# A two-layer linear-attention and MLP kernel on one core: a centred first tile, one more chunk divided in token order, two MLP tiles turned by DMA, and the orders arranged anew

## The chip, the core and the metric

The kernel runs on one core of one Trainium2 chip, in one launch. The core has five instruction streams: TensorE (PE, matmuls; its weight loads are shown apart as PEld), VectorE (DVE), ScalarE (ACT), GpSimd (POOL) and SyncE (SP), which here only issues DMAs. The metric is device time in microseconds (us), the median of the runs; lower is better. The profile is that of one more execution of the same program.

## What is computed

x is 2048 x 512 in bf16. Two layers follow one another, each an attention block and an MLP block with a residual, with the same weights in both layers:

```python
phi = lambda t: jnp.where(t > 0, t + 1, jnp.exp(t)) + 1e-6
def attention(x):                 # x is layer-normed, D = 512, 32 heads of 16
    q, k, v = heads(x @ wqkv)
    kv = einsum("sd,se->de", phi(k), v);  z = sum over s of phi(k)
    return (phi(q) @ kv / (phi(q) @ z + 1e-6)) @ wo
def mlp(x):                       # x is layer-normed, F = 1792
    return gelu_tanh(x @ w1 + b1) @ w2 + b2
for layer in range(2):
    x = x + attention(layernorm(x))
    x = x + mlp(layernorm(x))
```

Layer norm takes the mean off each row and divides by the root of the variance + 1e-5; there is no learned scale.

## The kernel before

**Tiles.** The 2048 rows are 16 tiles of 128 rows, in four chunks of four (tile 4c+k is the k-th of chunk c). A row tile is 128 x 512; matmuls contract over 128 partitions, so a product with a 512-deep weight is four matmuls into one PSUM bank, 512 columns each.

**Names.** The kernel first lists every operation as a node with a name, then plays the nodes, engine by engine, in an order that is written out by hand as long strings in `CONF["ORDER"]`. `CONF["PLACES"]` says which buffer slot each tile takes and who had it before, and `CONF["WAY"]` picks, operation by operation, the engine (`pe` or `dma` for a transpose, `dve`, `act` or `pool` elsewhere). From the data and slot dependences the waits are derived; nothing is scheduled at run time. The names that matter, with L the layer (0 or 1), t a tile, c a chunk:

| name | what | line |
|---|---|---|
| `warm` | matmuls on a constant while the first loads are under way | L747 |
| `stats`, `aggr`, `veps`, `pow`, `nmr`, `norm` + `A`/`B` L_t | layer norm ahead of attention (A) or of the MLP (B): row statistics (DVE), 1/sqrt(variance) (POOL), normalised tile in bf16 (DVE or ACT) | L773-L795 |
| `PT..`, `tc..` | a tile turned (128 x 128 blocks) on PE into PSUM, and copied out by ACT | L817, L827 |
| `T..`, `TP..` | a tile turned by a DMA that SP issues; TP turns a divided tile of queries | L804, L1067 |
| `K` L_t, `exp/relu/min/phi k..` | keys of a tile (4 matmuls), and phi of them into `pkb` | L866, L837-L854 |
| `Q` L_c_k | queries of a chunk: turned (L896), or in token order (L883) | |
| `G` | y^T phi(k), summed over all tiles; `KV` and `M` then multiply it by the weights of v and of `wo` | L958, L987, L1008, L1031 |
| `Z`, `zs`, `zb`, `dz`, `ZR` | the sums z and what is made of them | L941-L1022 |
| `D`, `ln`, `rec`, `pr` | the denominators of a chunk on turned queries: one matmul, then Ln and Exp(-) on ACT, then a product | L1074-L1082 |
| `pz`, `red`, `den`, `rec`, `pr` | the same in token order: a product with z, a sum per head, a reciprocal, a product (DVE, POOL), and then TP | L1051-L1067 |
| `WO`, `RA` | attention's output and its residual | L1097, L1102 |
| `W1`, `gelu`, `W2`, `RB`, `b2`, `OD` | the MLP, the residual, the bias, the store of a tile | L1127-L1175 |

**Stages.** Layer 0 begins with `warm`, while SP and ACT load x (tile 0 first, then tiles 1 to 3) and the weights of the keys. Tiles 0 to 5 are turned on PE, tiles 6 to 15 by DMA from SP's queue. A tile's K, phi and G follow; Q of chunks 0 and 1 fills PE. When the last tile is through, G is copied, and KV, M and the first WO form a chain through DVE and ACT, which Q of chunks 2 and 3 and the D matmuls fill. Chunks 2 and 3 are divided in token order, chunks 0 and 1 on turned queries. Then the MLP goes chunk by chunk, with W1 of chunk 0 in two halves of two tiles (256 columns), and a tile of layer 1 starts with its norm, T and K as soon as its RB is done. Layer 1 goes the same way (chunk 0 on turned queries, 1 to 3 in token order); there TB1_0 and TB1_1 are turned on PE and all other MLP tiles by DMA. The last row tile's W2 is done in two halves of 256 columns, so that its store can begin early.

**Queues.** SP issues its DMAs in the order of its string: a DMA that waits holds back those behind it. The late weights (`wv`, `wo`, `w1`, `w2`) are issued by POOL and wait until all of layer 0's first transposes have landed.

Of the kernel before, what the change touches and what calls it, by code (L numbers as in the profile page):

```python
# [1329 lines left out]
```

## Time and profile before

| | us |
|---|---|
| median of 3 runs (lowest, highest) | 328.95 (328.55, 329.53) |
| the profiled execution, its own time | 327.5 |
| its span, from the first to the last instruction | 326.3 |
| PE busy, of the span | 322.2 |
| DVE, ACT, POOL busy | 211.0, 193.1, 152.5 |
| granted TensorE clock, mean | 1.00 |

A line of a view by groups reads: line of the kernel, engine, operation, output<-inputs, partitions x elements, count; then busy time in all and the mean of one in ns; then the engine's idle time just before and what ended it. The chain of waits follows the work that ended last backwards: start, length, what. Matmuls are pipelined: the time from one to the next is shorter than the time that a row gives for one. Times in the views count from the start of the span.

### The profile page before, as it was taken

What the parts mean: (1) busy time and instruction counts of PE and PEld (TensorE: products, weight loads), DVE (VectorE), ACT (ScalarE), POOL (GpSimd) and SP (SyncE); (2) the same over time, 40 slices, a digit from 0 to 9 for tenths busy, and PEclk for the clock granted to TensorE, in tenths of its full rate; (3) what the DMA queues carried; (4) which work ended last, traced back from release to release, by engine and by line L of the source; (5) the groups of instructions that cost most, each with busy time, mean ns of one, the idle gap of its engine ahead of it and who ended that gap; (6) DMA issues with size and microseconds to landing.
All of it is one profiled execution on the core that took longest, in us unless ns stands there. A gap on an engine that the chain in (4) does not pass through costs nothing.

```text
span 326.3 us, 4763 instructions
## 1 busy us (share of the span) xinstructions
PE 322.2 (99%) x1723; PEld 159.3 (49%) x1723; DVE 211.0 (65%) x503; ACT 193.1 (59%) x334; POOL 152.5 (47%) x224
## 2 busy tenths in 40 slices
PE   8999999999999999999999999999999999999997
PEld 3444445576454444444444444458644444444444
DVE  5987679996938685142436899999989983300112
ACT  4988769797661416529673477969833454551600
POOL 5662548588663417300757434783856593100000
PEclk9999999999999999999999999999999999999999
DMA  7355753334012210331011110012034322200102
GB/s 266 120 83 97 219 189 104 105 64 68 16 32 50 54 26 3 80 64 34 0 32 33 34 32 0 19 32 50 17 82 94 69 48 66 64 0 2 64 0 80
DMA packets 46883, 20.37 MB, mean 62 GB/s; under 512 B 41932, under 2 KB 45388, under 8 KB 46860
## 3 DMA queue, kind: packets, MB, share of 16 engines
q1 hardware_dynamic: 44572, 13.00, 18.8%
q0 software_dynamic: 1056, 4.72, 4.5%
q10 hardware_dynamic: 1232, 2.36, 2.0%
q8 instruction: 13, 0.21, 0.3%
q14 instruction: 10, 0.08, 0.1%
HBM read 8.00 MB, written 2.10 MB: 31 GB/s over the span
## 4 chain that ended last, share of the span: by engine, by line
PE 97%; DVE 1%; ACT 1%; issue 0%
PE ps L1127 30%; PE ps L1163 29%; PE ps L1097 9%; PE ps L866 8%; PE ps L883 5%; PE ps L987 4%; PE ps L958 4%; PE ps L896 2%; PE ps L747 2%; PE ps L1150 1%; PE ps L1074 1%; PE ps L1008 1%; PE ps L1031 1%; PE ps L941 1%; PE ps L817 0%; DVE pkb L854 0%
## 5 line engine op out<-in xcount | busy, mean ns | idle before, releaser
L1132 ACT ACTIVATE gT<-ps,b1c 128x512 bf16<-128x512 f32 (+1 forms) x140 | 77.1, 600 | 65.3 <-PE ps L1127 65.0
L1127 PE MATMUL ps<-t,w 128*128 128x512 bf16 (+1 forms) x560 | 102.2, 336 | 0.0
L1163 PE MATMUL ps<-w,gT 128*128 128x512 bf16 x434 | 97.6, 379 | 0.0
L1127 PEld LDWEIGHTS ps<-t,w 128*128 128x128 bf16 x560 | 54.6, 98 | 43.7 <-ACT t L827 0.3
L1163 PEld LDWEIGHTS ps<-w,gT 128*128 128x128 bf16 x434 | 42.5, 98 | 50.4 <-DVE xsb L1169 0.2
L782 POOL TENSOR_TENSOR rstd<-veps,neghalf 128x1 f32<-128x1 f32 x64 | 37.9, 602 | 33.5 <-DVE veps L780 31.4
L837 ACT ACTIVATE eb<-ps 128x512 bf16<-128x512 f32 x64 | 37.4, 614 | 18.3 <-PE ps L866 10.5
L1173 DVE TENSOR_TENSOR outb<-ps,xsb 128x512 bf16<-128x512 f32 x15 | 10.1, 686 | 46.3 <-PE ps L1163 40.3
L773 DVE BATCH_NORM_STATS2 stats<-xsb 128x6 f32<-128x512 f32 x48 | 32.3, 678 | 0.4
L848 ACT ACTIVATE rb<-ps 128x512 bf16<-128x512 f32 x45 | 26.6, 617 | 9.2 <-PE ps L866 8.7
L866 PE MATMUL ps<-wqkv,t 128*128 128x512 bf16 x128 | 31.6, 379 | 0.1
L1097 PE MATMUL ps<-gtb,t 128*128 128x512 bf16 x128 | 31.2, 379 | 0.1
L850 DVE TENSOR_SCALAR eb<-eb 128x512 bf16<-128x512 bf16 x45 | 14.0, 321 | 21.1 <-ACT eb L837 21.1
L1113 POOL TENSOR_TENSOR xsb<-xsb,b2b 128x512 f32<-128x512 f32 x20 | 24.3, 1224 | 6.8 <-ACT yb L790 6.6
L790 ACT ACTIVATE yb<-xsb,nmr,rstd 128x512 bf16<-128x512 f32 x21 | 16.7, 812 | 14.2 <-POOL nmr L787 13.9
L780 POOL TENSOR_SCALAR veps<-mv 128x1 f32<-128x1 f32 x35 | 7.6, 217 | 30.8 <-DVE mv L775 28.1
L1063 POOL TENSOR_TENSOR t<-t,rr 128x512 bf16<-128x512 bf16 x14 | 15.5, 1114 | 13.6 <-DVE rr L1059 12.9
L795 DVE TENSOR_SCALAR yb<-xsb,mv,rstd 128x512 bf16<-128x512 f32 x27 | 16.1, 602 | 8.5 <-POOL rstd L782 8.3
L1051 POOL TENSOR_TENSOR lr<-t,zrow 128x512 f32<-128x512 bf16 x15 | 17.9, 1191 | 5.7 <-ACT zrow L971 4.2
L883 PE MATMUL ps<-wqkv,t 128*128 128x512 bf16 x80 | 19.9, 379 | 0.0
L1097 PEld LDWEIGHTS ps<-gtb,t 128*128 128x128 bf16 x128 | 12.3, 98 | 14.7 <-DVE rr L1059 0.6
L866 PEld LDWEIGHTS ps<-wqkv,t 128*128 128x128 bf16 x128 | 12.0, 98 | 14.9 <-ACT t L827 1.0
(97 smaller groups left out, 373.5 us busy)
## 6 DMA issues: line engine op xcount, KB each, us to landing
w<-in_B_w_dram POOLq DMA_DIRECT2D x4, 896.0 KB, 6.9
out_dram<-outb SPq DMA_DIRECT2D x15, 128.0 KB, 1.9
t<-in_A_x_dram ACTq DMA_DIRECT2D x3, 512.0 KB, 4.6
t<-yb SPq DMA_TRANSPOSE x56, 2.5
wqkv<-in_A_wqkv_dram ACTq DMA_DIRECT2D x1, 512.0 KB, 5.8
wqkv<-in_A_wqkv_dram POOLq DMA_DIRECT2D x1, 512.0 KB, 4.6
wo<-in_A_wo_dram POOLq DMA_DIRECT2D x1, 512.0 KB, 5.5
t<-in_A_x_dram SPq DMA_DIRECT2D x1, 384.0 KB, 3.1
```

What stands on the lines that cost most here:

```text
L773: G.op("dve", lambda e: e.bn_stats(stats[:, s.slot, :], src()), 620, reads=src_keys, writes=[k + "s"], tiles=[s, *src_tiles], name=f"stats ...
L782: G.op("pool", lambda e: e.tensor_tensor(rstd[:, s.slot:s.slot + 1], veps[:, s.slot:s.slot + 1], neghalf[:], op=ALU.pow), 570, reads=[k + ...
L837: G.op("act", lambda e: e.activation(eb[:, et.slot, :], bank(bt), ACT.Exp), 478, reads=[src_key], writes=[f"e{tag}"], tiles=[bt, et], name ...
L848: G.op("act", lambda e: e.activation(rb[:, rt.slot, :], bank(bt), ACT.Relu), 478, reads=[src_key], writes=[f"r{tag}"], tiles=[bt, rt], nam ...
L866: ins = e.matmul(bank(b), lhsT=yTa(yT)[:, dt, k * P:(k + 1) * P], rhs=wqkv[:, dt, D:2 * D], start=(dt == 0), stop=(dt == DT - 1))
L883: ins = e.matmul(bank(b), lhsT=yTa(yT)[:, dt, k * P:(k + 1) * P], rhs=wqkv[:, dt, 0:D], start=(dt == 0), stop=(dt == DT - 1))
L1051: lambda e, r=r, tok=tok: e.tensor_tensor(lr[:, r.slot, :], tok(), zrow[:], op=ALU.mult), 1150 if on_pool else 600,
L1097: ins = e.matmul(bank(wb), lhsT=yTa(pq)[:, kt, k * P:(k + 1) * P], rhs=gtb[:, kt, :], start=(kt == 0), stop=(kt == DT - 1))
L1113: G.op("pool" if on_pool else "dve", lambda e: e.tensor_tensor(xsb[:, st, :], xsb[:, st, :], b2b[:], op=ALU.add), 1120 if on_pool else 600 ...
L1127: ins = e.matmul(bank(b, n), lhsT=w1[:, dt, ft * P:(ft + 1) * P], rhs=yTa(yT)[:, dt, k0 * P:k1 * P], start=(dt == 0), stop=(dt == DT - 1))
L1132: G.op("act", lambda e, ft=ft, b=b, k0=k0, k1=k1, n=n: e.activation(gT[:, g.slot, ft * 512 + k0 * P:ft * 512 + k1 * P], bank(b, n), ACT.Ge ...
L1163: ins = e.matmul(bank(b), lhsT=gT[:, g.slot, ft * 512 + k * P:ft * 512 + (k + 1) * P], rhs=w2[:, ft, :], start=(ft == 0), stop=(ft == FT - 1))
```

## The change

1. **Tile 0** is also centred (mean taken off, no scale) as soon as its mean is there; this centred tile is turned on PE (`PTC0`, `tcC0`) and K0_0 is made of it. The scale 1/sqrt(variance) is applied afterwards, as the `scale` operand of K0_0's Exp and Relu. The fully normed tile 0 is still made, for G and Q, and turned by DMA (`TA0_0`).
2. **Chunk 1 of layer 0** is divided in token order (`den0_1: tok`): Q0_1 is made in token order, four D matmuls, four Ln and four Exp go, and `pz`, `red`, `den`, `rec`, `pr` and TP0_1 come.
3. **TB1_0 and TB1_1** are turned by DMA, and so are tiles 4 and 5 of layer 0 (`TA0_4`, `TA0_5`).
4. The warm matmuls become 7 of 512 columns and 8 of 256, which stand around `PTC0` (before: 15 of 512).
5. The last tile's W2 is cut into 384 and 128 columns, the 128 first.
6. `b1` and `b2` are loaded after all first transposes, not after the first.
7. All five orders, the slots and many choices of an engine are new. DVE has 536 operations (503), ACT 313 (325), POOL 204 (220), SP 108 (99). DVE has 20 of the `b2` additions (12), 8 of the `za` additions (1) and 11 of the `pz` products (5). ACT changes its function table 14 times (12).

The functions' part of the diff, cut to its core:

```diff
-    WARM=[[512, 512, 512, 512, 512, 512, 512, 512, 512, 512, 512], [512, 512, 512, 512]],
+    WARM=[[512, 512, 512, 512, 512, 512, 512], [256], [256], [256], [256], [256], [256], [256], [256]],
...
+            mean = lambda: stats[:, s.slot, 2:3] if by_act else mv[:, s.slot, 0:1]
+            if centred is not None:
+                yc = Tile(YB, f"yc{tag}")
+                G.op("dve", lambda e: e.tensor_scalar(yb[:, yc.slot, :], src(), mean(), None, op0=ALU.add if by_act else ALU.subtract),
+                     300, reads=[k + "m", *src_keys], writes=[f"yc{tag}"], tiles=[s, yc, *src_tiles], name=f"cen{tag}", lat=40, fast=True)
...
-            G.op("act", lambda e: e.activation(eb[:, et.slot, :], bank(bt), ACT.Exp), 478, ...
+            by = (lambda: 1.0) if scaled is None else (lambda: rstd[:, scaled[0].slot:scaled[0].slot + 1])
+            G.op("act", lambda e: e.activation(eb[:, et.slot, :], bank(bt), ACT.Exp, scale=by()), 478, ...
-            G.op("act", lambda e: e.activation(rb[:, rt.slot, :], bank(bt), ACT.Relu), 478, ...
+            G.op("act", lambda e: e.activation(rb[:, rt.slot, :], bank(bt), ACT.Relu, scale=by()), 478, ...
...
-                for h in range(2):
+                for h, (c0, c1) in enumerate(((0, 3 * P), (3 * P, D))):
...
+                if cen:
+                    yTc = yTc or Tile(T4, f"yTc{c}")
+                    yc, yckey, sc, sckey = cen[0]
+                    transpose_pe(yc, yckey, yTc, k, f"yTc{st}", f"C{st}", True)
+                    tr = transpose(y, ykey, yT, k, f"yT0_{st}", f"A0_{st}")
...
+                pk = attn_k(0, c, k, yTc, f"yTc{st}", (sc, sckey)) if cen else attn_k(0, c, k, yT)
```

The heads of the two strings of orders (`...` for what is left out):

```diff
 "pe"
-warm0 warm1 PTA0_0 PTA0_1 K0_0 PTA0_2 K0_1 PTA0_3 K0_2 PTA0_4 G0_0_0 K0_3 K0_4 Q0_0_0 G0_1_0 PTA0_5 ...
+warm0 warm7 warm6 warm5 PTC0 warm4 warm3 warm2 warm8 warm1 K0_0 PTA0_2 PTA0_1 K0_2 PTA0_3 K0_1 G0_0_0 K0_3 Q0_0_2 ...
 "sp"
-x0 x1 wk0 TA0_7 TA0_6 TA0_8 TA0_14 TA0_15 TA0_13 TA0_12 b2 TA0_10 TA0_11 TA0_9 b1 Tb1 TB0_1 TB0_0 ...
+x0 x1 wk0 TA0_0 TA0_4 TA0_5 TA0_7 TA0_13 TA0_6 TA0_12 TA0_14 TA0_15 TA0_8 TA0_9 TA0_10 TA0_11 b1 Tb1 b2 TP0_1_3 ...
```

Layer 1's first WO tiles, up to W1: before `WO1_2_0 Q1_2_2 WO1_3_0 WO1_5_0 WO1_4_0 PTB1_1 Q1_2_3 PTB1_0 WO1_6_0`, after `WO1_1_0 Q1_2_1 WO1_2_0 WO1_6_0 Q1_3_3 WO1_3_0 Q1_2_2 Q1_2_3 WO1_5_0 WO1_4_0`. Layer 0's, from WO0_1 to W1: before eight products with four Q between them, after eight with two Q; two of the four Q stand ahead of KV instead.

More of the change, by code (lines that the diff above doesn't have):

```diff
@@ L794, in norm @@
             else:
-                G.op("dve", lambda e: e.tensor_scalar(yb[:, y.slot, :], src(), stats[:, s.slot, 2:3] if by_act else mv[:, s.slot, 0:1],
+                G.op("dve", lambda e: e.tensor_scalar(yb[:, y.slot, :], src(), mean(),
                                                       rstd[:, s.slot:s.slot + 1], op0=ALU.add if by_act else ALU.subtract, op1=ALU.mult),
@@ L832, in yTa, with phi @@
             return t4[:, yT.slot, :].rearrange("p (d s) -> p d s", d=DT)
-        def phi(bt, src_key, dst, dst_key, dst_tiles, tag):
+        def phi(bt, src_key, dst, dst_key, dst_tiles, tag, scaled=None):
             et = Tile(EB, f"e{tag}")
-            G.op("act", lambda e: e.activation(eb[:, et.slot, :], bank(bt), ACT.Exp), 478, reads=[src_key], writes=[f"e{tag}"],
-                 tiles=[bt, et], name=f"exp{tag}", lat=90, table="exp")
-            if eng(f"phi{tag}") == "max":
+            by = (lambda: 1.0) if scaled is None else (lambda: rstd[:, scaled[0].slot:scaled[0].slot + 1])
+            more_tiles, more_keys = ([], []) if scaled is None else ([scaled[0]], [scaled[1]])
+            G.op("act", lambda e: e.activation(eb[:, et.slot, :], bank(bt), ACT.Exp, scale=by()), 478, reads=[src_key, *more_keys],
+                 writes=[f"e{tag}"], tiles=[bt, et, *more_tiles], name=f"exp{tag}", lat=90, table="exp")
+            if eng(f"phi{tag}") == "max" and scaled is None:
                 G.op("dve", lambda e: e.tensor_scalar(eb[:, et.slot, :], eb[:, et.slot, :], 1.0, 1e-6, op0=ALU.min, op1=ALU.add),
@@ L847, in phi @@
             rt = Tile(RB, f"r{tag}")
-            G.op("act", lambda e: e.activation(rb[:, rt.slot, :], bank(bt), ACT.Relu), 478, reads=[src_key], writes=[f"r{tag}"],
-                 tiles=[bt, rt], name=f"relu{tag}", lat=90)
+            G.op("act", lambda e: e.activation(rb[:, rt.slot, :], bank(bt), ACT.Relu, scale=by()), 478, reads=[src_key, *more_keys],
+                 writes=[f"r{tag}"], tiles=[bt, rt, *more_tiles], name=f"relu{tag}", lat=90)
             G.op("dve", lambda e: e.tensor_scalar(eb[:, et.slot, :], eb[:, et.slot, :], 1.0, 1e-6, op0=ALU.min, op1=ALU.add),
@@ L856, in phi, with attn_k @@
                  name=f"phi{tag}", lat=60, fast=not on_pool)
-        def attn_k(L, c, k, yT):
+        def attn_k(L, c, k, yT, key=None, scaled=None):
             st = 4 * c + k
@@ L862, in attn_k, with fn @@
             pk = Tile(PK, f"pk{L}_{st}")
-            def fn(e):
-                for dt in range(DT):
-                    ins = e.matmul(bank(b), lhsT=yTa(yT)[:, dt, k * P:(k + 1) * P], rhs=wqkv[:, dt, D:2 * D],
-                                   start=(dt == 0), stop=(dt == DT - 1))
-                return ins
-            G.op("pe", fn, 4 * MM, reads=[f"yT{L}_{st}", "wk"], writes=[f"k{L}_{st}"], tiles=[b, yT],
-                 name=f"K{L}_{st}", lat=MM_DRAIN, n=4)
-            phi(b, f"k{L}_{st}", lambda: pkb[:, pk.slot, :], f"pk{L}_{st}", [pk], f"k{L}_{st}")
+            halves = eng(f"ks{st}") if L == 0 else None
+            parts = [(2, 3), (0, 1)] if halves else [tuple(range(DT))]
+            for i, part in enumerate(parts):
+                def fn(e, i=i, part=part):
+                    for n, dt in enumerate(part):
+                        ins = e.matmul(bank(b), lhsT=yTa(yT)[:, dt, k * P:(k + 1) * P], rhs=wqkv[:, dt, D:2 * D],
+                                       start=(i == 0 and n == 0), stop=(i == len(parts) - 1 and n == len(part) - 1))
+                    return ins
+                G.op("pe", fn, len(part) * MM, reads=[key or f"yT{L}_{st}", *[f"wk_{dt}" for dt in part]] + ([f"k{L}_{st}"] if i else []),
+                     writes=[f"k{L}_{st}"], tiles=[b, yT], name=f"K{L}_{st}" + "ab"[i] * (len(parts) > 1), lat=MM_DRAIN, n=len(part))
+            phi(b, f"k{L}_{st}", lambda: pkb[:, pk.slot, :], f"pk{L}_{st}", [pk], f"k{L}_{st}", scaled)
             return pk
@@ L1143, in mlp_down, with fn @@
                 ot = Tile(OUT, f"out{st}")
[L1144 removed]
+                for h, (c0, c1) in enumerate(((0, 3 * P), (3 * P, D))):
                     hb = b if h == 0 else Tile(psum, f"w{L}_{st}_h", "w")
[L1146 to L1148 removed]
+                    cs = slice(c0, c1)
+                    def fn(e, hb=hb, cs=cs, n=c1 - c0):
                         for ft in range(FT):
[L1150 removed]
+                            ins = e.matmul(bank(hb, n), lhsT=gT[:, g.slot, ft * 512 + k * P:ft * 512 + (k + 1) * P], rhs=w2[:, ft, cs],
                                            start=(ft == 0), stop=(ft == FT - 1))
                         return ins
[L1153 removed]
+                    n = c1 - c0
+                    G.op("pe", fn, FT * (n / 2.4 + 2.5), reads=[f"g{L}_{c}_{ft}_{k}" for ft in range(FT)] + ["w2"], writes=[f"w{L}_{st}_{h}"],
                          tiles=[hb, g], name=f"W2{L}_{st}_h{h}", lat=MM_DRAIN, n=FT)
[L1155 to L1156 removed]
+                    G.op("dve", lambda e, hb=hb, cs=cs, n=n: e.tensor_tensor(outb[:, ot.slot, cs], bank(hb, n), xsb[:, st, cs], op=ALU.add),
+                         60 + n * 1.06, reads=[f"w{L}_{st}_{h}", ("x", st)], writes=[f"out{st}_{h}"], tiles=[hb, ot], name=f"RB{L}_{st}_{h}", lat=60)
                     dma("sp", lambda e, cs=cs: e.dma_start(rows(out_dram, c)[:, k, cs], outb[:, ot.slot, cs]), [f"od{st}_{h}"],
[L1158 removed]
+                        tiles=[ot], reads=[f"out{st}_{h}"], name=f"OD{st}_{h}", sem=f"d_out_h{h}", kb=n // 4)
                 return
@@ L1204, in build_kernel @@
             attn_q(0, c, yT, pq)
+        dma("sp", lambda e: e.dma_start(b1r[0:FT, :], B_b1.rearrange("(ft p) -> ft p", p=P)), ["b1r"], name="b1", kb=4, after=trs)
+        dma("sp", lambda e: e.dma_start(b2b[:], bass.AP(B_b2.tensor, B_b2.offset, [[0, P], [1, D]])), ["b2b"], name="b2", kb=128, after=trs)
+        consts()
         late("wv", "wv", wqkv[:, :, 2 * D:3 * D], wsrc[:, :, 2 * D:3 * D], 512, trs)
```

24 lines of the change are left out of this document (7 added, 17 removed), and 552 rows, old and new, of tables (ORDER, PLACES, WAY).

## The prediction, on record before the changed kernel ran

> **What bounds the kernel now.** I read the page first: busy shares, then the chain of work that ended last.
>
> ```profile
> span 326.3 us, 4763 instructions
> PE 322.2 (99%) x1723; PEld 159.3 (49%) x1723; DVE 211.0 (65%) x503; ACT 193.1 (59%) x334; POOL 152.5 (47%) x224
> ...
> PE   8999999999999999999999999999999999999997
> ...
> PEclk9999999999999999999999999999999999999999
> ...
> PE 97%; DVE 1%; ACT 1%; issue 0%
> ```
>
> PE is the bound from end to end: 97% of the chain, no slice below full but the first and the last. So a microsecond taken out of PE's own list is a microsecond of the time, as long as no other engine is late for PE; work that moves between DVE, ACT and POOL costs nothing until then. What PE loses is in few places, and the chain in order of time shows them (start, length, what):
>
> ```profile
> 0.84 6.34 PE ps L747 x15
> 7.17 0.24 PE ps L817 x4
> 7.41 0.02 issue
> 7.43 0.60 ACT t L827
> 8.04 0.05 issue
> 8.09 1.04 PE ps L866 x4
> 9.12 0.22 PE ps L817 x4
> 9.35 0.86 PE ps L866 x4
> ...
> 42.15 0.22 PE ps L1074
> ...
> 216.96 0.26 PE ps L817 x4
> ...
> 218.08 0.22 PE ps L817 x4
> ...
> 250.42 0.13 issue
> 250.56 1.02 PE ps L1097 x4
> ...
> 322.61 1.54 PE ps L1150 x14
> 324.15 0.02 issue
> 324.17 0.42 DVE outb L1155
> ```
>
> The first product of use (K0_0, L866) starts at 8.09. A tile turned on PE is 0.22, a D matmul 0.22, a product of four 0.86. Longer waits are rare; the view of waits has the one that counts ahead of G:
>
> ```profile
> PE ps L941 <- DVE pkb L854: 0.7, 1, 0.7
> ```
>
> **The change, part by part.** The profiled execution took 327.5, its span is 326.3; the median of the runs is 328.95, 1.45 above. The terms are differences against the profiled execution, and I put them on the median.
>
> *The start.* The timeline has the chain to K0_0 and what the new one is made of:
>
> ```profile
> 1.72 0.43 SPq L706 DMA_DIRECT2D wqkv<-in_A_wqkv_dram  x1
> 3.94 0.18 DVE L775 BATCH_NORM_AGGREGATE mv<-stats 128x2 f32<-128x6 f32 x1
> 4.16 0.15 DVE L780 TENSOR_SCALAR veps<-mv 128x1 f32<-128x1 f32 x1
> 4.39 0.56 POOL L782 TENSOR_TENSOR rstd<-veps,neghalf 128x1 f32<-128x1 f32 x1 [0.80 <-DVE veps L780]
> 4.99 0.41 DVE L795 TENSOR_SCALAR yb<-t,mv,rstd 128x512 bf16<-128x512 bf16 x1 [0.68 <-POOL rstd L782]
> 5.32 0.69 DVE L773 BATCH_NORM_STATS2 stats<-t 128x6 f32<-128x512 bf16 x1
> ```
>
> ```profile
> wqkv<-in_A_wqkv_dram SPq DMA_DIRECT2D x1, 256.0 KB, 4.5
> ```
>
> Before, tile 0 is normed at 5.40, but the 15 warm matmuls hold PE to 7.0. After, the centring needs neither `veps` nor `pow`: it runs 4.16 to about 4.57. Seven warm matmuls of 0.42 (6.34 / 15) end at 3.8, three halves at 4.5, so PTC0 goes at 4.6, its copy (0.60) ends near 5.85, and five more halves last to 6.1. Then the load of the keys' weights binds: 1.72 + 4.5 = 6.2. **K0_0 starts at 6.3, 1.8 earlier.** Not all of that stays, for tile 2 is next: its statistics follow the centring (4.5 + 0.69 + 0.18 = 5.4), POOL's `veps` and `pow` take 0.8 (6.3), the norm 0.41 (6.75); but PE is in K0_0 to about 7.35, turns the tile to 7.6, drains at 7.8, ACT copies to 8.4. The second K starts at 8.45, against 9.35, with 0.65 idle on PE ahead of it. I take **-0.9**; from -1.8, if nothing behind K0_0 were late, to +0.3, if the clock is late (second rival).
>
> What follows K0_0 is scaled in ACT; no row has that form. The nearest are without and with two pointer operands:
>
> ```profile
> L837 ACT ACTIVATE eb<-ps 128x512 bf16<-128x512 f32 x64 | 37.4, 614 | 18.3 <-PE ps L866 10.5
> ...
> L790 ACT ACTIVATE yb<-xsb,nmr,rstd 128x512 bf16<-128x512 f32 x21 | 16.7, 812 | 14.2 <-POOL nmr L787 13.9
> ```
>
> So the two operations cost 0 to 0.2 more each; I take half, 0.2 for both. They delay G0_0_0, for which PE comes at 10.4 and phi at about 10.5: 0.1 that I leave in the small waits below. (The Trainium skill, "ScalarE: Activation LUTs", section "What ACT_TABLE_LOAD costs", gives about 93 ns for each pointer operand, an estimate of 0.19 for the two; the sum would be the same.)
>
> *Tiles 4 and 5 by DMA*: two turns of 0.22 leave PE, **-0.44**. ACT is rid of two copies, SP's queue gets three transposes more (13, with TA0_0), and begins at 7 instead of 15:
>
> ```profile
> 15.35 11.40 SPq L804 DMA_TRANSPOSE t<-yb  x7
> ...
> 27.43 4.40 SPq L804 DMA_TRANSPOSE t<-yb  x3
> ```
>
> ```profile
> t<-yb SPq DMA_TRANSPOSE x56, 2.5
> ```
>
> One takes at most 1.47 of the queue (4.40 / 3) and lands 2.5 after issue. I walked the new order through with these durations: the first is issued near 7.1, tile 12's near 22, tile 11's near 30 and it lands at 32.5, when PE comes to K0_11 at 32.7. It holds, with 0.2 to spare; third rival.
>
> *The old wait of 0.7 ahead of Z0_2* (phi of the last tile was late) goes: the new order has G0_7, Q0_0_3 and Q0_1_1 between the last K and Z0_3, and my walk has phi there in time. With two 0.1 gaps around it: **-0.8** (0 to -1.0).
>
> *Chunk 1 in token order*: four D matmuls go, **-0.86** (4 x 0.216). Q0_1 stays four products of 0.86. Ln and Exp leave ACT, which is no bound; the work comes to DVE and POOL between the last G and WO0_0,
>
> ```profile
> L1054 DVE TENSOR_REDUCE rd<-lr 128x32 f32<-128x512 f32 x20 | 13.5, 675 | 3.7 <-POOL lr L1051 3.6
> ...
> L1059 DVE RECIPROCAL rr<-rd 128x32 f32<-128x32 f32 x20 | 6.6, 336 | 0.1
> ```
>
> four times 0.68 + 0.34 and small ones, some 4.5 on DVE in a stretch where PE has 14, next to KV and M. These queue ahead of `cpg` and `kvm`; PE has two Q (1.7) more to fill the gap there. From WO0_0's end PE has two Q less until W1 (10.4 before minus 1.7 = 8.6), while the new chain, with rows as above, is RA 0.68, statistics, pow, norm 0.55 for two tiles and 2.5 for the turn: 7.6 to 8.0. It fits with half a microsecond. I cost it at nothing; if that cover fails, each 0.1 that the norm is late is 0.1 of the time.
>
> *TB1_0 and TB1_1 by DMA*: **-0.48** (0.26 + 0.22). PE has ten products (8.6) between WO1_0 and W1 where it had seven and two turns (6.5); the chain with two landings is about 8.0. Covered, by 0.6.
>
> *The gap at 250* (0.13, and 0.16 in the 1.02 that should be 0.86): WO1_15 waited for a transpose that SP issued late; the new queue is other work in another order, **-0.3** (0 to -0.3).
>
> *The tail*: the last product is 384 columns, and the VectorE addition behind it grows by half of the step from 0.42 (256) to 0.69 (512), 0.13, its store by little: **+0.2**. The slot of its output waits for a store that is issued about 3 us earlier and lands in 1.9; if that binds, +0.7.
>
> *Moves between the engines*: 33 more operations on DVE, 16 fewer on POOL. Two more table loads on ACT (1.28 each) fall between K1 and the gelu of chunk 3, when ACT waits for PE anyway. Nothing, as long as DVE is in time; fourth rival. *b1, b2 later*: read first near 60; nothing. *New small waits*: the old order had waits of the size of the 0.7 and the 0.16 quoted, and the new one, as worked out above, is full of covers of 0.2 to 0.6; I take one such wait back, **+0.6** (0 to +3).
>
> Sum: -0.9 - 0.44 - 0.8 - 0.86 - 0.48 - 0.3 + 0.2 + 0.6 = **-2.98**. The profiled execution would be 324.5, and the median **326.0**.
>
> **The rivals.** *First, the forecast.* PE stays the bound, its list is about 1.8 shorter behind K0_0, and it starts earlier.
>
> *Second: the clock comes late.* The rows show that the 15 warm matmuls ran at 0.42 each, and that K0_0, after 6 us of them, ran at 0.22 a matmul. Now the warm work is 4.7 us with a turn in it, and K0_0 starts 5.5 after the first. If PE is still at half rate until 10.2, K0_0 lasts 1.7, two turns 0.9, and the second K begins at 9.25, half of it slow: G0_0_0 is 1.2 later than forecast, 327.2. Against it: PE is as full as before up to 6.3. (The Trainium skill, "TensorE: Matmul & The Clock Gate", part 1, says that the clock is let go after a busy window of about 3.4 us that runs freely, and part 4 that a transpose does not count as busy. By the first alone the clock comes between 3.4 and 6.8 us after the first matmul, and the trace's 6 agrees; by the second, PTC0 could spoil a window, and the sum would be this rival's 327.2.)
>
> *Third: the waits come back.* PE is some 2.5 us ahead of the old times from 10 on, and the transposes, ACT or DVE don't follow. If a transpose takes 1.6 of the queue (11.40 / 7) instead of 1.35, the six behind tile 12's are 1.7 late, K0_11 waits 1.5, and a second place of this kind (KV1_3, behind copies on two engines) some 0.5: 328.0.
>
> *Fourth, slower: DVE becomes the bound of layer 1's start.* The view by stretches:
>
> ```profile
> 188.40:267.90 79.50, 79.37 (x463) 41.84 (x461) 72.24 (x171) 54.01 (x98) 49.61 (x63) 1.00 0.21 44
> ```
>
> ```profile
> L1113 DVE TENSOR_TENSOR xsb<-xsb,b2b 128x512 f32<-128x512 f32 x12 | 11.9, 999 | 0.0
> ```
>
> DVE is busy 72.2 of 79.5 there. The new order has three additions of the bias more in it, up to 1.0 each when POOL is at the same memory, and one RB; and za, nine and more operations of 0.7, ahead of it. If the stretch starts with DVE 5 late, it needs 72 + 4 + 5 = 81 busy against 78 of PE's work, and the norms of chunks 1 to 3 are late for W1: with the covers of about 3 gone, PE idles 5 to 6 in all: 331. It decides from the point at which DVE is more than 3 behind PE at RA1_0. Against it: in the 180 us before, DVE is far from full, so it should not be behind.
>
> **How the numbers follow.** Forecast 0.61 (325.0 to 327.2), late clock 0.12, waits back 0.17, DVE 0.10. About 0.3% (1.0) is what a measurement of this kernel can tell from no change: 328.0 to 329.9. Of the waits' case 0.07 lies above 328.0, and 0.03 of the forecast's: faster 0.80, same 0.10, slower 0.10. The range leaves out DVE's 0.10 and as much at its ends: down to 324.2 (no new waits, and half of the 0.9 that K0_0 lost comes back), up to 328.8.
>
> **What would show it.** K0_0 at 6.3, the second K at 8.45 with 0.65 of PE idle ahead; matmuls of 0.22 from there (else the second rival). G0_10 some 2.4 earlier than before, the first W1 product near 60.6 instead of 63.98, layer 1's near 215.2 instead of 219.16. A PE wait at K0_10 or K0_11 on a transpose is the third rival; PE idle between 195 and 265 with DVE full the fourth. If PE's list is not 1.5 to 1.9 shorter after K0_0, the count is wrong.

## The result, and the profile after

| | before | after |
|---|---|---|
| median (lowest, highest), us | 328.9 (328.55, 329.53) | 326.21 (325.33, 326.42) |
| ratio, 95% interval | | 0.9911 (0.9887, 0.9935) |
| the profiled execution, its span | 327.5, 326.3 | 326.31, 325.1 |
| PE's products from K0_0 on, by count | 314.4 | 312.9 |
| PE's waits from K0_0 on | 1.65 | 3.53 |
| last matmul's end to the last landing | 2.07 | 2.36 |

Faster by 2.7 by the medians, where 2.95 was forecast. But the two profiled executions differ by 1.2 only, and the rest of this document goes by them, so the close hit is not yet an explanation. In the last three rows products, waits and the tail are taken from PE's instructions one by one: each product's columns at the spacing of PE's row (0.216 for 512), and what is left between two products.

The page of the changed kernel:

```profile
span 325.1 us, 4707 instructions
PE 316.7 (97%) x1673; PEld 157.2 (48%) x1703; DVE 219.3 (67%) x536; ACT 188.9 (58%) x324; POOL 134.9 (42%) x208
...
PE   7899999998999999999999999999999999999997
...
DVE  6987799989897496029349899999886843101103
...
PE 87%; DVE 4%; ACT 3%; DMA 3%; issue 1%; POOL 1%; SPq 0%
```

(30 matmul records are missing from this trace, 1673 of 1703, which is why PE's busy time looks smaller.) PE was 97% of the chain and is 87% now: the chain runs through transfers, VectorE and ACT where they are just in time for PE or late. Between the first slice and the last, two are below full, the second and the tenth. The chain in order of time shows the second:

```profile
1.71 4.47 DMA wqkv<-in_A_wqkv_dram
6.17 0.09 issue
6.26 1.02 PE ps L879 x4
...
9.82 0.42 DVE pkb L864
10.24 0.32 DVE yb L803
10.57 0.03 DVE mv L777
10.60 4.26 DMA t<-yb
14.85 0.14 issue
14.99 1.02 PE ps L879 x4
```

K0_0 starts at 6.26 and waits for the keys' weights, as forecast. Then tile 4 (the `t<-yb` here) is issued at 10.60 and lands 4.26 later; PE, which was ready for K0_4 at 13.8, waits 1.2. The tenth slice:

```profile
78.45 0.45 PE ps L1140 x4
78.90 0.02 issue
78.92 0.48 ACT gT L1145
79.41 1.02 issue
80.43 1.67 PE ps L1140 x7
```

W10_1_5_0, the first product of chunk 1's W1, starts at 80.43, 1.27 after PE could. The view of waits names no releaser (`issue`); by the semaphores it is the turn TB0_5, issued at 76.02 and landed at 80.34. The two old waits are gone: Z0_2 waits 0.03 (it was 0.80), and there is none at 250 (it was 0.30).

The ledger of the profiled pair: K0_0 -1.82, list -1.54 (one turn has moved from ahead of K0_0 to behind it, 0.22), waits +1.88, tail +0.29: -1.19.

### The profile page after: what moved, and what is told of

It reads as the page before. It is cut to its first block, busy times and chain, and to the rows that moved or that the text cites. A ratio compares the mean times of both kernels' runs of the same rounds, so it can differ in the third digit from the quotient of the medians.

```text
span 325.1 us, 4707 instructions
## 1 busy us (share of the span) xinstructions
PE 316.7 (97%) x1673; PEld 157.2 (48%) x1703; DVE 219.3 (67%) x536; ACT 188.9 (58%) x324; POOL 134.9 (42%) x208
## 3 DMA queue, kind: packets, MB, share of 16 engines
q10 hardware_dynamic: 1232, 2.36, 2.2%
## 4 chain that ended last, share of the span: by engine, by line
PE 87%; DVE 4%; ACT 3%; DMA 3%; issue 1%; POOL 1%; SPq 0%
PE ps L1177 28%; PE ps L1140 27%; PE ps L879 8%; PE ps L1110 7%; PE ps L896 6%; PE ps L971 4%; PE ps L1000 3%; PE ps L909 2%; DVE xsb L1115 1%; DMA wqkv<-in_A_wqkv_dram 1%; DMA t<-yb 1%; DVE stats L775 1%; PE ps L1163 1%; ACT L1303 1%; ACT gT L1145 1%
## 5 line engine op out<-in xcount | busy, mean ns | idle before, releaser
L1140 PEld LDWEIGHTS ps<-t,w 128*128 128x128 bf16 x560 | 54.6, 98 | 45.5 <-ACT gT L1145 1.6
L879 PE MATMUL ps<-wqkv,t 128*128 128x512 bf16 x125 | 30.6, 379 | 2.2 <-DMA t<-yb 1.1
L1110 PE MATMUL ps<-gtb,t 128*128 128x512 bf16 x124 | 30.4, 379 | 0.2
L1076 POOL TENSOR_TENSOR t<-t,rr 128x512 bf16<-128x512 bf16 x18 | 19.9, 1114 | 11.3 <-DVE rr L1072 7.6
L896 PE MATMUL ps<-wqkv,t 128*128 128x512 bf16 x95 | 23.6, 379 | 0.1
L1183 DVE TENSOR_TENSOR xsb<-ps,xsb 128x512 f32<-128x512 f32 x16 | 10.8, 679 | 14.7 <-PE ps L1177 14.7
L1110 PEld LDWEIGHTS ps<-gtb,t 128*128 128x128 bf16 x128 | 12.4, 98 | 14.5 <-issue 0.3
L1064 POOL TENSOR_TENSOR lr<-t,zrow 128x512 f32<-128x512 bf16 x13 | 14.9, 1153 | 9.9 <-ACT zrow L984 3.7
L1126 DVE TENSOR_TENSOR xsb<-xsb,b2b 128x512 f32<-128x512 f32 x20 | 14.4, 730 | 5.2 <-ACT yb L798 5.2
L803 DVE TENSOR_SCALAR yb<-xsb,mv,rstd 128x512 bf16<-128x512 f32 x27 | 15.1, 566 | 3.1 <-POOL rstd L784 2.1
```

The source lines that it names most:

```text
L879: ins = e.matmul(bank(b), lhsT=yTa(yT)[:, dt, k * P:(k + 1) * P], rhs=wqkv[:, dt, D:2 * D], start=(i == 0 and n == 0), stop=(i == len(part ...
L896: ins = e.matmul(bank(b), lhsT=yTa(yT)[:, dt, k * P:(k + 1) * P], rhs=wqkv[:, dt, 0:D], start=(dt == 0), stop=(dt == DT - 1))
L1076: lambda e, d=d, tok=tok, heads=heads: e.tensor_tensor(heads(tok()), heads(tok()), rr[:, d.slot, :].unsqueeze(2).broadcast_to([P, H, DH]), ...
L1110: ins = e.matmul(bank(wb), lhsT=yTa(pq)[:, kt, k * P:(k + 1) * P], rhs=gtb[:, kt, :], start=(kt == 0), stop=(kt == DT - 1))
L1140: ins = e.matmul(bank(b, n), lhsT=w1[:, dt, ft * P:(ft + 1) * P], rhs=yTa(yT)[:, dt, k0 * P:k1 * P], start=(dt == 0), stop=(dt == DT - 1))
```

## The experiments

All kernels are timed against the kernel before on the same chip. Medians of the kernel before there: 329.56 in the first four runs, 329.09 in the next four, 329.23 in the last four, which ran on another chip.

| run | median | ratio (95%) | span of its profile | K0_0 | waits from K0_0 on |
|---|---|---|---|---|---|
| after_again | 326.77 | 0.991 (0.9874, 0.9945) | 325.6 | 6.14 | 4.20 |
| before_again (one time) | 328.43 | | 327.2 | 7.84 | 2.84 |
| xc2_later | 325.61 | 0.987 (0.9826, 0.9914) | 324.4 | 6.55 | 2.53 |
| t4_pe | 325.98 | 0.9888 (0.9849, 0.9927) | 324.7 | 6.07 | 3.14 |
| b_warm11 | 329.02 | 0.999 (0.9969, 1.0011) | 326.9 | 7.81 | 2.61 |
| cen_off_x | 325.74 | 0.9884 (0.9858, 0.991) | 323.7 | 7.49 | 0.98 |
| tok_off | 327.58 | 0.9956 (0.9933, 0.9978) | 325.6 | 6.19 | 3.32 |
| fetch_shift | 326.19 | 0.9895 (0.9871, 0.992) | 324.8 | 6.44 | 2.44 |
| less_warm_tail | 325.65 | 0.9888 (0.9872, 0.9905) | 323.4 | 6.34 | 2.04 |
| b_start | 328.86 | 0.9998 (0.9981, 1.0015) | 327.6 | 6.53 | 4.30 |
| tok_off2 | 328.32 | 0.9977 (0.9954, 1.0001) | 327.4 | 6.16 | 5.13 |
| tb1_pe | 326.59 | 0.9937 (0.9915, 0.9959) | 324.4 | 6.62 | 1.95 |

### Both kernels once more: after_again, before_again

No edit.

> The changed kernel once more, nothing edited. Theory: its profile has two waits that the sum did not have, 1.22 us ahead of K0_4 (the turn of tile 4 by DMA lands 4.26 after its issue, beside the loads of wq and x's third chunk) and 1.27 ahead of W10_1_5_0 (TB0_5 lands 4.32 after its issue, with a fetch of instructions between). If both belong to the kernel they stand in this profile too, within 0.3, and the median is 326.0 to 326.5. Rival: they are chance of one execution; then this profile lacks one or both and its own time is 1 to 2 lower.

> The kernel before once more, nothing edited. Its profiled execution took 327.5 where the median of its runs is 328.9; the after kernel's took 326.3 at a median of 326.2. Theory: the executions of before differ by DMA landings, and the shown profile was a lucky one: this profile has 0.5 to 1.5 more of PE waits than the 1.65 of the shown one, and a time of 328 to 329.3. Rival: the profiler's run is shorter in itself by 1.4 for this kernel: 327.3 to 327.8 again, with the same waits.

Both long waits are there again, the first in another shape: tile 0's turn, which Q0_0_2 needs, lands 6.16 after its issue and PE waits 1.57 for it, and tile 4's lands 4.88 after its issue, for which K0_4 waits 0.28 more. W10_1_5_0 waits 1.30. The kernel before had 1.2 more of waits than in the profile shown, and took 328.43. In all it was timed 65 times here, from 327.38 to 331.01, and one of these times lies below the shown 327.5. So the shown profile of before was a lucky execution, and a difference of profiles understates the change: 1.2 by the first pair, 1.6 (spans 327.2 and 325.6) by the second, 2.7 and 2.8 by the medians. What the slower executions of before do in the remaining 1 us isn't shown by any profile here.

### The loads and tile 4: xc2_later, t4_pe

```diff
 "act"
-... expk0_1 xc2 reluk0_1 expk0_3 reluk0_3 ...
+... expk0_1 reluk0_1 expk0_3 xc2 reluk0_3 ...
```

> The load of x's third chunk is issued by ACT three operations later (about 12.9 instead of 10.4), behind the turn of tile 4 and not beside it; nothing else moves. Theory (the loads hold the turn up): TA0_4 lands about 2.5 after its issue at 10.6, so near 13.1, K0_4 runs when PE comes to it at 13.8, its wait of 1.2 goes, and the time is 0.8 to 1.2 below the after kernel, near 325.2, unless the third chunk's tiles are then late. Rival (turns on this queue are slow at this point for another reason, or the wait comes back at K0_10): TA0_4 still lands after 14.5, or the time stays within 0.3 of the after kernel.

```diff
-"TA0_4": "dma",
+"TA0_4": "pe",
 "pe"
-... G0_0_0 K0_3 Q0_0_2 Q0_0_0 K0_4 ...
+... G0_0_0 PTA0_4 K0_3 Q0_0_0 Q0_0_2 K0_4 ...
 "act"
-... reluk0_1 expk0_3 ...
+... reluk0_1 tcA0_4 expk0_3 ...
 "sp"
-... TA0_0 TA0_4 TA0_5 ...
+... TA0_0 TA0_5 ...
```

> Tile 4 is turned on PE again, as before the change (0.22 on PE, a copy on ACT; Q0_0_0 and Q0_0_2 change places). Theory: the wait of 1.2 ahead of K0_4 goes and PE gets 0.22 more: 0.8 to 1.0 below the after kernel, near 325.3, the same as with the later load less 0.2. Rival (PE's lead is taken back at the next tile whose turn is late, K0_5, K0_10 or Z0_2): the time stays within 0.3 of the after kernel, with the wait at another place.

On the same chip, after_again took 326.77, xc2_later 325.61 and t4_pe 325.98: 1.16 and 0.79 less, as the theory says. (For t4_pe that is weak: its runs go from 324.48 to 326.39 and those of after_again from 325.40 to 327.60.) The view of DMAs around the issue of TA0_4, first of the changed kernel (10.55 to 12.0), then of xc2_later (11.2 to 12.4):

```profile
t<-in_A_x_dram ACTq DMA_DIRECT2D x1, 512.0 KB, 3.8
t<-yb SPq DMA_TRANSPOSE x1, 4.3
```

```profile
t<-yb SPq DMA_TRANSPOSE x1, 2.4
```

The same turn takes 4.3 with the 512 KB load of x's third chunk issued beside it, and 2.4 without; K0_4 waits no more. The load now stands beside the next turn, TA0_5, which lands 3.2 after its issue instead of 2.45, but PE needs that one later and doesn't wait. In t4_pe the wait is gone too, but another came, at W10_0_11_0:

```profile
PE ps L1140 <- DMA t<-yb: 1.5, 1, 1.5
```

while the one at W10_1_5_0 was not there. Only the four matmuls of one turn and a copy had come in, 50 us earlier. The view of DMAs from 58.5 to 62.8 shows what the late turn (TB0_1, landed 4.15 after its issue) met:

```profile
q8 instruction: 1, 0.02, 1.4%
...
t<-yb SPq DMA_TRANSPOSE x2, 3.3
```

### Packets of instructions: fetch_shift

In every profile here a packet of 16 KB comes on the queue that the page calls q8 instruction, in the changed kernel after the first 79 matmuls of PE and then every 108 to 148. In the changed kernel one comes at 77.93 and takes 1.36. The view of DMAs from 75.9 to 80.5, where a digit is 0.115 us:

```profile
DMA  2999982000007999990000049999910100000000
...
q8 instruction: 1, 0.02, 1.9%
...
t<-yb SPq DMA_TRANSPOSE x2, 3.4
```

Two bursts of 0.7 are turns (TB0_4 up to 76.7, TB0_5 from 77.4 to 78.0), and a third at 78.7 belongs to TP0_2_0. Then there is a long trickle up to 80.3 (under a tenth, so 0 in the row), and only there TB0_5 lands. One of its 16 shares is behind: in the trace its semaphore is raised 15 times between 78.37 and 78.48, which is 2.35 to 2.46 after the issue, and the last time at 80.34.

```diff
-WARM=[[512, 512, 512, 512, 512, 512, 512], [256], [256], [256], [256], [256], [256], [256], [256]],
+WARM=[[512] * 7] + [[64, 48, 48, 48, 48]] * 8,
```

> The changed kernel with the later load (base 325.6), and the eight warm matmuls of 256 columns cut into five pieces each of the same sum: 32 matmuls and weight loads more in PE's program, the same columns. In every profile so far a 16 KB packet of an instruction queue comes about every 120 matmuls of PE, and a DMA turn that meets one lands 3.2 to 4.4 us after its issue instead of 2.5; in the base the one at 77.6 meets TB0_5, for which W10_1_5_0 waits 1.0. Theory (these packets are fetches of PE's instructions and make the turn late): all packets come about 32 matmuls earlier, the one of 77.6 at 70 to 74, TB0_5 lands in 2.5 to 2.7, the wait at W10_1_5_0 falls under 0.3, and the time is 0.7 to 1.0 below the base unless another packet now meets a turn that is needed at once. Rival (TB0_5 is late because of the queue or VectorE at that place): it still lands over 4 after its issue and the wait stays.

The packets of 19.0, 61.7 and 77.6 of the base come at 16.0, 53.5 and 72.5 (the one of 39.2 at 38.2). They move with an edit of PE's program alone, so they are taken to be its instructions being fetched. TB0_5 lands 2.5 after its issue, and W10_1_5_0 waits 0.24 instead of 1.01. The view of DMAs from 74.5 to 79.1, and the chain there:

```profile
t<-yb SPq DMA_TRANSPOSE x3, 2.5
```

```profile
79.18 0.02 issue
79.20 0.48 ACT gT L1145
79.68 1.87 PE ps L1140 x8
```

But the time is not lower (326.19, 0.6 above the base, where 0.7 to 1.0 below was expected). The packet of 16.0 now meets TA0_5, which the expectation left open as "another packet": it lands at 18.51, 4.92 after its issue, and K0_5 waits 0.87. (The view of waits names an Exp of ACT for it, but K0_5's first weight load starts at 18.61, ahead of the end of that Exp at 18.64, and the bank had been free since 17.0.) The load of x's third chunk stands beside this turn as well; in the base the turn landed 3.21 after its issue beside that load alone, and K0_5 did not wait. The view of DMAs from 13.4 to 18.6:

```profile
q8 instruction: 1, 0.02, 1.1%
...
t<-yb SPq DMA_TRANSPOSE x3, 3.5
```

A second loss is at the end: a packet comes at 318.95, the two stores issued at 318.53 and 318.90 land after 2.5 and 2.8 (1.9 and 2.0 in the base), VectorE waits for their slots, and from the last matmul to the last landing it is 3.04 instead of 2.37. So the mechanism is shown by the landings, and the gain was lost at two other places, both beside such a packet.

All fourteen profiles agree at TB0_5. In seven a packet of 16 KB begins 1.2 to 2.1 after its issue, and it lands after 4.1 to 4.4; in the other seven none does, and it lands after 2.5 (in two of them one begins 2.2 and 2.4 after the issue, when the turn is all but done). The kernel before is among the first seven: its TB0_5 landed after 4.27, and PE did not wait for it. In the changed kernel 7 of the 85 turns land 3.0 to 4.4 after their issue: five were under way when one of the 16 KB packets began, two when one of 8 KB on another instruction queue (q14) did. But ten more met one of 8 KB and landed in 2.4 to 2.7, so a small packet need not matter. Two turns are late beside the first loads; the others have 2.4 to 2.6.

### The start: b_warm11, cen_off_x, b_start

```diff
 kernel before
-    WARM=[[512, 512, 512, 512, 512, 512, 512, 512, 512, 512, 512], [512, 512, 512, 512]],
+    WARM=[[512] * 7, [512] * 4],
```

> The kernel before with 11 warm matmuls instead of 15, nothing else. The prediction put the earlier start down to the centring. Rival: the old start was held by its own warm matmuls (to 7.0, with tile 0 normed at 5.4), and fewer of them give most of it: the turn of tile 0 at about 5.5, its copy to 6.3, K0_0 at 6.4 to 6.6 instead of 8.1. By the rival K0_0 starts before 6.8 and the time is 0.6 to 1.6 below the kernel before, as far as no late clock (a matmul over 0.3 us behind K0_0) takes it back. By the prediction's view (the centring is what makes it early) K0_0 stays above 7.3 and the time within 0.4.

This told nothing on its question. PE stood in PTA0_1, which is ahead of K0_0 in the old order and needs tile 1's norm, and ACT in the squares of tile 3: K0_0 came at 7.81, and the time stayed.

```diff
 base: xc2_later
-"cen0": "1",  "vepsA0_0": "pool",
+"vepsA0_0": "dve",
 "dve"
-... aggrA0_0 cenA0_0 statsA0_2 ... normA0_2 normA0_0 normA0_1 ...
+... aggrA0_0 vepsA0_0 statsA0_2 normA0_0 ... normA0_2 normA0_1 ...
 "pe"
-warm0 warm7 warm6 warm5 PTC0 warm4 warm3 warm2 warm8 warm1 K0_0 ...
+warm0 warm7 warm6 warm5 warm4 warm3 warm2 warm8 PTA0_0 warm1 K0_0 ...
 "act"
-... sumA0_3 tcC0 xc3 sqA0_3 wq ...
+... sumA0_3 xc3 sqA0_3 tcA0_0 wq ...
 "sp"
-... wk0 TA0_0 TA0_4 ...
+... wk0 TA0_4 ...
```

> The changed kernel with the later load of x's third chunk (the run of that name is its base, 325.6), and tile 0 no longer centred: normed before its turn on PE, no scale in Exp and Relu, no DMA turn of it; the shorter warm work stays. By the prediction the centring gives the start: K0_0 comes 0.5 or more later than in the base, and the time is 0.5 to 0.9 above it. Rival (the shorter warm work gives it, the loads of the keys' weights bind at 6.2 anyway): K0_0 at 6.4 to 6.7, the time within 0.3 of the base.

K0_0 in the timeline of PE, of the base and then of cen_off_x (start, length, what, and in brackets the idle time before it):

```profile
6.55 1.04 PE L879 MATMUL ps<-wqkv,t 128*128 128x512 bf16 x4 [1.01 <-ACT t L835]
```

```profile
7.49 1.04 PE L879 MATMUL ps<-wqkv,t 128*128 128x512 bf16 x4 [0.92 <-ACT t L835]
```

Without the centring K0_0 comes 0.94 later (a copy on ACT stands behind the squares), as the prediction has it, and the time is the same (325.74 against 325.61), as the rival has it. Neither was right on both. PE was 0.94 later at K0_0 and 0.40 later at G0_10_0, but W10_1_5_0, for which the base waited, no longer waited: the lead that the base had was spent there. That was the packets' doing: in the base one met TB0_5 (landed after 4.23), here none did (2.49). So whether the 0.40 would last without that packet isn't shown.

```diff
 kernel before
-    WARM=[[512, 512, 512, 512, 512, 512, 512, 512, 512, 512, 512], [512, 512, 512, 512]],
+    WARM=[[512] * 7, [512] * 4],
 "pe"
-warm0 warm1 PTA0_0 PTA0_1 K0_0 ...
+warm0 warm1 PTA0_0 K0_0 PTA0_1 ...
 "act"
-... sqA0_3 tcA0_0 ...
+... tcA0_0 sqA0_3 ...
```

> The kernel before with only its start mended, without centring: 11 warm matmuls, PTA0_1 behind K0_0 on PE, tile 0's copy ahead of tile 3's squares on ACT (in the run with 11 alone PE stood in PTA0_1, and ACT in the squares, ahead of K0_0). Theory of the runs so far: centring isn't needed, K0_0 starts at 6.4 to 6.7, as in the changed kernel; but the lead is lost again at waits for turns and norms in the first 40 us and at W10_1_1_0, so that the time falls by less: 0 to 0.8 below the kernel before. The prediction's view (0.9 of the lead stays): 0.7 to 1.1 below the kernel before.

K0_0 comes at 6.53 without centring, 1.56 earlier than in the shown profile of before, and the time is that of the kernel before. PE then waits 1.20 ahead of PTA0_2 and 1.46 ahead of K0_6, whose turn meets two packets of instructions. The chain of b_start from 6 to 22 says who leads there:

```profile
by line: DVE stats L773 30.5%; DMA t<-in_A_x_dram 28.1%; DMA t<-yb 26.2%; DVE yb L795 10.4%; DVE eb L850 5.3%; DVE mv L775 5.2%; PE ps L866 5.0%; DVE pkb L854 4.2%; DVE eb L841 1.3%; issue 1.1%; DVE veps L780 0.7%
...
12.22 1.79 DVE stats L773 x3
...
16.94 4.19 DMA t<-yb
```

Loads, VectorE's statistics and turns, with PE 5% of the chain. G0_0_0 starts at 11.39, against 11.40 in the shown profile of before: the lead of 1.56 is gone there already, ahead of any packet. In the old order an earlier K0_0 alone was worth nothing.

### Chunk 1 on turned queries again: tok_off, tok_off2

```diff
 base: xc2_later
-"den0_1": "tok",
 "pe"
+D0_1_0 behind G0_12_0, D0_1_1 behind D0_0_3, D0_1_2 behind Q0_3_0, D0_1_3 behind WO0_0_3
-WO0_2_0 WO0_7_0 Q0_2_3 Q0_3_2
+WO0_2_0 Q0_2_3 Q0_3_2 WO0_7_0
 "act"
+ln0_1_0 rec0_1_0 ln0_1_1 rec0_1_1 behind rec0_0_3, ln0_1_2 rec0_1_2 ln0_1_3 rec0_1_3 behind expq0_2_1
 "dve", "pool", "sp"
-pz0_1, red0_1, den0_1, rec0_1, TP0_1
+pr0_1_3 on VectorE
 tok_off2 besides: reluq0_3_0 expq0_3_0 ahead of ln0_1_2; pr0_1_2 on VectorE
```

> The changed kernel with the later load (base 325.6), and chunk 1 of layer 0 divided on turned queries as before the change: four D matmuls (0.86), four Ln and four Exp come back, pz, red, den, rec and four DMA turns go; WO0_7 stands behind two Q. By the prediction (PE binds, the divisions lie beside it) the time is 0.7 to 1.0 above the base. Rival (the 4.5 us that the token order adds on VectorE are what makes chunk 1's norms late, and so the wait of 1.0 at W10_1_5_0): that wait goes with the change undone and the time is within 0.3 of the base.

> Chunk 1 of layer 0 on turned queries, on the base with the later load (325.6), once more: in the first try WO0_3_0 waited 1.8 for a bank that Relu and Exp of Q0_3_0 held, behind the Ln and Exp that came back. Now these two stand ahead of them on ACT, and two of the products are VectorE's. By the prediction (0.86 of PE, nothing else) the time is 0.6 to 1.1 above the base, with no wait over 0.4 at WO0_3_0. By the rival (VectorE's 4.5 us more are what makes W10_1_5_0 wait, so the token order gives little) that wait of 1.0 goes and the time is within 0.3 of the base.

PE's list is 0.86 longer in both (313.72 against 312.86), as counted. The times are 2.0 and (on the other chip) 2.7 above the base, too much for either theory, and the profiles show why: the edits made waits of their own. In tok_off WO0_3_0 waits 1.78 for a bank; in tok_off2 D0_1_3 waits 0.85 for Ln, which shares its bank, the queries wait 1.25 ahead of Q0_0_2 for TA0_0 (landed 6.0 after its issue), and WO0_7_0, W10_0_11_0 and WO0_8_0 wait 1.4 together. The wait at W10_1_5_0 is gone in both, but PE is 2 to 3 us later there and no packet met TB0_5, so that tells nothing of VectorE. The 0.86 is shown as PE's work; what the token order costs elsewhere stays open.

### The MLP turns and the tail: tb1_pe, less_warm_tail

```diff
 base: xc2_later
-"TB1_0": "dma", "TB1_1": "dma",
+"TB1_0": "pe", "TB1_1": "pe",
 "pe"
-... WO1_3_0 Q1_2_2 Q1_2_3 WO1_5_0 ...
+... WO1_3_0 PTB1_0 Q1_2_2 Q1_2_3 PTB1_1 WO1_5_0 ...
```

(with the two copies on ACT, and without the two DMAs)

> TB1_0 and TB1_1 turned on PE again, on the base with the later load (325.6). By the prediction (0.48 of PE's list, the turns by DMA covered by 0.6) layer 1's first W1 product comes 0.4 to 0.5 later than in the base, relative to WO1_0, and the time rises by as much. Rival (the turn of TB1_1 lands 0.07 ahead of that product, so the chain of norm and turn binds there and not PE; turning on PE makes it shorter): the product comes 0 to 0.3 later, the time within 0.3 of the base.

From WO1_0 to the first W1 product it takes 9.50 in the base (207.64 to 217.14) and 9.94 here (206.74 to 216.68): 0.44 more, of 0.48 counted. The median is 1.0 above that of the base, on another chip. The prediction's step holds, but not its cover of 0.6: in the base TB1_1 lands 0.08 ahead of the product that needs it, and in the changed kernel (landed at 217.80) the product waits 0.15.

```diff
 base: xc2_later
-WARM=[[512, 512, 512, 512, 512, 512, 512], [256], [256], [256], [256], [256], [256], [256], [256]],
+WARM=[[512] * 7, [512], [512], [256]],
-for h, (c0, c1) in enumerate(((0, 3 * P), (3 * P, D))):
+for h, (c0, c1) in enumerate(((0, 2 * P), (2 * P, D))):
 "pe"
-warm0 warm7 warm6 warm5 PTC0 warm4 warm3 warm2 warm8 warm1 K0_0 ...
+warm0 warm3 warm1 PTC0 warm2 K0_0 ...
```

> The changed kernel with the later load (base 325.6), and two edits that the profiles can tell apart: the eight warm matmuls of 256 columns become two of 512 and one of 256 (five matmuls less in PE's program, and fewer columns), and the last tile's W2 is cut 256/256 again. Theory of the fetches: the packets come about five matmuls, 0.7 us, later, the one of 77.6 at 78.2 to 78.5, just behind TB0_5's landing (75.6 + 2.5 = 78.1); the wait of 1.0 at W10_1_5_0 falls under 0.3. Tail: from the last matmul's end to the last landing 2.08 again, not 2.36. Together 0.8 to 1.3 below the base: 324.3 to 324.8. Rival: TB0_5 is still late, or another turn meets a packet (K0_5, W10_0_11_0), or the clock falls back in the pause ahead of K0_0: the time within 0.4 of the base.

The profile does what was expected: no wait at W10_1_5_0, and the tail of before again. The last pieces of the chain, of the changed kernel and of this one:

```profile
319.60 3.07 PE ps L1163 x28
322.67 0.02 issue
322.69 0.56 DVE outb L1169
```

```profile
318.20 3.07 PE ps L1162 x28
321.27 0.02 issue
321.30 0.42 DVE outb L1168
```

The last addition is 0.56 or 0.42, and from the last matmul to the last landing it is 2.36 or 2.08. But the way to W10_1_5_0 was another one: the packet came at 77.33 and not later, and TB0_5 got by because the whole kernel was 0.4 earlier there than in the base (issued at 75.12, landed 2.49 later). This profile has the lowest span of all, 323.4, and its execution took 324.63; the median of its four runs is 325.65, no better than the base's. xc2_later (0.987) and less_warm_tail (0.9888) both have lower medians than the changed kernel (0.991 in two series), but the intervals overlap; within one series, xc2_later is 1.16 below it.

## Why the prediction was right, point by point

| step | forecast | the profiles |
|---|---|---|
| K0_0 | 6.3 | 6.26 |
| second K | 8.45, PE idle 0.65 | 8.20, idle 0.62 ahead of it |
| the start, as far as it lasts | -0.9 | -1.09 at G0_0_0; nothing left at K0_4 (+1.2 of wait) |
| tiles 4 and 5 off PE | -0.44 | -0.44 of the list, and the wait at K0_4 |
| Z0_2 | -0.8 | -0.77 |
| D0_1 | -0.86 | -0.86 of the list |
| TB1_0, TB1_1 | -0.48 | -0.45 of the list, 0.44 in tb1_pe |
| gap at 250 | -0.3 | -0.30 |
| tail | +0.2 | +0.29 |
| new small waits | +0.6 | about 2.2 |
| one turn moved behind K0_0 | not counted | +0.22 of the list |
| sum | -2.98 | -1.2 (profiles), -2.7 (medians) |
| start of G0_10 | 2.4 earlier | 0.96 earlier (41.12, 40.16) |
| first W1 product, layer 0 | 3.4 earlier | 2.0 earlier (63.81, 61.77) |
| first W1 product, layer 1 | 4.0 earlier | 1.2 earlier (219.00, 217.84) |

The last three rows are signs that the prediction named; matmul starts, before and after. Of the lead that was forecast, 1.0 of 2.4 is there at G0_10, 2.0 of 3.4 at layer 0's first W1, and 1.2 of 4.0 at layer 1's.

**Right:** what bounds the kernel, the count of PE's list (but for the turn that moved), the start up to G0_0_0, the waits that go, the tail. **Not borne out:** the late clock (K0_0's four matmuls take 1.02) and a VectorE-bound layer 1.

**Mis-sized: the new waits.** The step "I take one such wait back, +0.6 (0 to +3)" stood for 2.2: K0_4 and W10_1_5_0 make 2.5, and the small ones elsewhere are 0.3 less than before. The step "One takes at most 1.47 of the queue (4.40 / 3) and lands 2.5 after issue" took the median landing of the whole kernel; beside a load a turn took 4.3, and xc2_later shows the difference. (Most turns hold SP for 1.2 to 1.4, so 1.47 was enough for them; three beside a packet held it for 1.9 to 2.4.) The profile of before held such a turn: TA0_10, issued at 27.43 beside the load of `b2`, landed 4.06 later.

The wait at W10_1_5_0 was in no step. It is the third rival's mechanism at a place it didn't name: PE came there 2.0 us earlier (it was ready at 79.16, where before it came at 81.20), and the last turn that it needs landed only 0.5 earlier (80.34, before 80.87). 2.47 after its issue, as usual, TB0_5 would have landed at 78.5, ahead of PE: the cover of 0.7 was less than the 1.85 that the packet added. What set its issue at 76.02 is in the timeline (the two norms of VectorE are tiles 4 and 5, that of ACT is tile 6, the three transposes are TB0_6, TB0_4 and TB0_5):

```profile
72.45 0.80 ACT L798 ACTIVATE yb<-xsb,nmr,rstd 128x512 bf16<-128x512 f32 x1
72.45 1.89 DVE L803 TENSOR_SCALAR yb<-xsb,mv,rstd 128x512 bf16<-128x512 f32 x2 [0.44 <-POOL rstd L784]
...
73.28 4.00 SPq L812 DMA_TRANSPOSE t<-yb  x3
```

The norm behind TB0_5 was done at 74.34, 1.7 ahead of its issue. SP issued TB0_6 when ACT's norm was done (73.25), then TB0_4 and TB0_5 one behind the other, 1.3 to 1.4 each. VectorE did get fuller, as the view by stretches shows (before, then after; behind the stretch's length stand the busy times of PE, PE's weight loads and VectorE):

```profile
41.00:63.80 22.80, 22.80 (x119) 10.69 (x118) 20.12 (x44) 18.82 (x34) 13.27 (x14) 1.00 0.46 139
63.80:97.00 33.20, 33.20 (x211) 20.48 (x210) 25.34 (x62) 24.70 (x47) 25.21 (x30) 1.00 0.25 44
```

```profile
40.00:61.80 21.80, 21.69 (x113) 10.27 (x114) 20.79 (x46) 13.22 (x25) 15.74 (x18) 1.00 0.67 221
61.80:96.00 34.20, 32.94 (x203) 19.89 (x206) 31.77 (x79) 24.98 (x46) 17.03 (x22) 1.00 0.22 43
```

From 40 to 96 it went from 45.5 busy of 56.0 to 52.6 of 56.0: the fourth rival looked for this in layer 1, and it is in layer 0, where chunk 1's divisions and moved work came to it. But it is not what TB0_5 waited for last; VectorE itself stood idle 0.44 for POOL ahead of these norms. Whether its load delayed the statistics further back isn't shown.

**Wrong: the step from profile to median.** "The terms are differences against the profiled execution, and I put them on the median" took the 1.45 between them as constant. It is not: the changed kernel's profiled execution lies on its median. The sum of -2.98 should have been about -1.2 to -1.6 by the profiles, and the median moved by 2.7 since the kernel before is usually slower than its profile. So 326.0 came out by two errors of about 1.4 that cancel, which is luck.

**Not shown in its reason: the start.** K0_0 comes 1.8 earlier, but no time of a run shows that the centring makes the kernel faster: cen_off_x has the same time without it (though a packet spared it a wait that its base had), and b_start has nearly the same K0_0 and no gain. In the profiles the centring is worth 0.94 at K0_0 and 0.40 at G0_10. What the lead is worth is set by VectorE's statistics, the loads and the turns of the tiles behind.

## What to carry to other kernels

A microsecond taken from the bound engine's list is worth a microsecond only up to the next place where another chain is due: walk the lead to each such place, and take a DMA's duration from rows with the same traffic beside it. A profile is one execution; before a difference of profiles is put on a median, look how far the profiled execution lies from the runs of both kernels. Where a critical transfer takes 1 to 2 us longer than its like, look for a packet of an instruction queue in the same moment: adding or removing a few matmuls anywhere before moves it, so that small edits shift the time by about 1 us for no reason of their own.
